# The tail of an FFT convolution kernel: reload in two portions, the last put on another queue, evictions of two banks, six outputs

## The chip, the cores and the metric

The kernel runs on one core of one Trainium2 chip. The metric is the device time of one execution in microseconds (us). Three runs of the kernel before took 263.7, 263.68 and 265.46 us, so their median is 263.7 us. The profile comes from one further execution.

## The reference

The input `x` is 1 x 224 x 224 x 96 and the filter `w` is 7 x 7 x 96 x 96, both bf16. The reference multiplies their two-dimensional spectra and transforms back, which is a circular convolution over the whole image:

```python
wp = jnp.pad(w, ((0, H - K), (0, W - K), (0, 0), (0, 0)))
Xf = rfft2(x.astype(float32), axes=(1, 2))
Wf = rfft2(wp.astype(float32), axes=(0, 1))
Yf = jnp.einsum('bhwi,hwio->bhwo', Xf, Wf)
y  = irfft2(Yf, s=(H, W), axes=(1, 2)).astype(bfloat16)
```

## The kernel before

**Tiling.** The kernel transforms along the height alone, in 8 blocks (`NJ`) of 28 output rows (`B`), to 17 frequencies (`NS`) with a real and an imaginary part each. Along the width it works directly with 7 taps, in 7 tiles (`NT`) of 32 columns, which it treats as 16 pairs (`TW`) in even and odd phase. The last tile has the index 6 (`TL`).

**Stages.** For each tile, matmuls with `Fm` take `x` to frequencies (`xf`), and VectorE makes sums and differences of them (`J`, in `jit`). `b_round(t, s, ...)` then does the products of one frequency `s`: some 33 matmuls of 96 columns into two PSUM banks, a ScalarE evacuation of the first bank (`tt__`), two VectorE operations (`u`, `v`), and a sum `yf` on GpSimd or, in some rounds, on VectorE. One round takes some 1.4 us. Every three frequencies (two at the end), the `yf` tile is written to DRAM scratch (a "put"), since the transform back needs the frequencies on the partitions. Scratch is then read back in that order in pieces of 384 bytes, multiplied by `G` (`tt` and `Gm` in the profile), evacuated by ScalarE and VectorE into `yo` or `J`, and sent to the output (`c_jobs`). For all tiles but the last, this happens in the shade of the products of later tiles.

**The last tile.** Its transform back can't lie behind another tile. Its scratch is cut at the frequencies of `SLAST` = (0, 9, 12, 15, 17). The part 0 to 9 (`scra`) is reloaded by two transfers of 480 KB when round 11 is reached (`s == SA + 2`); the parts 9 to 12, 12 to 15 and 15 to 17 (`scrb`) are reloaded by `load_b` after the last round. The puts of the last tile are collected in `puts` and issued from ScalarE's queue in a later round, except the last one, which SyncE issues. After the rounds, 12 more matmuls with `Gm` of the tile before are evacuated (the loop over `cj`). Then come

- 8 matmuls with `GA` on the first part (`first`), each 384 columns into a bank of its own;
- 26 matmuls on zeros (`WARM`) that add nothing;
- 16 matmuls with `GB` on the second part (`second`), which complete the sums, with the remaining 8 of `first` between them. Each is evacuated by `tail_evac` on one of the two engines, and each pair of 384 columns leaves as an output of 168 KB, eight outputs in all.

**Order.** The class `_Ordered` (line 89) makes each engine run its instructions in the order in which the program makes them. All compute instructions are recorded by the helper at line 99, and so all carry that line in the profile. Transfers carry one of eight completion semaphores in turn; an engine that issues a transfer first waits until the transfer that had the same semaphore before it has landed.

Of the kernel before, what the change touches and what calls it, by code (L numbers as in the profile page):

```python
# [8 lines left out]
BF16 = mybir.dt.bfloat16  # L9
F32 = mybir.dt.float32  # L10
# [4 lines left out]
B = 28  # L15
L = B + KT - 1
LC = L - 2
NS = L // 2
REAL = (0, NS - 1)
JG = 4  # L20
NJ = 8
# [12 lines left out]
PGRP = ((0, 5), (5, 8), (8, 11), (11, 14), (14, 17))  # L34
YGRP = ((0, 3), (3, 6), (6, 9), (9, 12), (12, 15), (15, 17))
YGRPL = ((0, 3), (3, 6), (6, 9), (9, 12), (12, 15), (15, 17))
SLAST = (0, 9, 12, 15, 17)
SA = SLAST[1]
YMAX = 3
YBUF = 4  # L40
JGB = ((0, 3), (3, 6), (6, 9), (9, 12), (12, 15), (15, 17))
# [23 lines left out]
def kernel(  # L65
# [50 lines left out]
    def bank():  # L116
        return pools["psb"].tile([128, 512], F32, name="pb")
# [27 lines left out]
        load["a"] += ca  # L145
        return SE.copy(out=out_ap, in_=in_ap)

    def dma(out_ap, in_ap):
        return DE.dma_start(out=out_ap, in_=in_ap)

    WF = cpool.tile([128, NSLOT, NTAP, C], BF16, name="WF")
    PP = POS * NJ
# [2 lines left out]
    xf_bufs = [cpool.tile([128, 2, 2, NS, POS, NJ], BF16, name=f"xf{i}") for i in range(2)]  # L155
    Fm = cpool.tile([R, 2, NS, JG], BF16, name="Fm")
    G = cpool.tile([3 * FR, 3 * B], BF16, name="Gm")
    KA = 4 * 2 * SA
    NL = len(SLAST) - 1
    KB = [NJ * 2 * (SLAST[i + 1] - SLAST[i]) for i in range(1, NL)]  # L160
    RB = [sum(KB[:i]) for i in range(NL - 1)]
    assert sum(KB) == 128
    XW = 2 * TW * C
    xn_bufs = [cpool.tile([R, XW + 32], BF16, name=f"xn{i}") for i in range(2)]
# [430 lines left out]
    def b_round(t, s, mid, end, ydve=False, planes=()):  # L595
# [90 lines left out]
        if s == y1 - 1:  # L686
            dst, yo0 = scr_tiles[t], 0
            if t == TL:
                i = sum(s >= v for v in SLAST[1:])
                dst, yo0 = scr_tiles[(t, i)], SLAST[i]  # L690

            def put(eng=DE):
                eng.dma_start(out=dst.rearrange("w j s e -> (w j) s e")[:, y0 - yo0:y1 - yo0],
                              in_=yf[:, 0:y1 - y0].rearrange("p s r m o -> p s (r m o)"))
            if t == TL and s < NS - 1:
                puts.append(lambda: put(SE))
            else:
                put()
# [17 lines left out]

    TW2 = 2 * TW * C
    tl_all = xf_bufs[(TL + 1) % 2].rearrange("c p r s w j -> c (p r s w j)")
    KAP = -(-KA // 16) * 16
    tl_a = [tl_all[0:KAP, g * TW2:(g + 1) * TW2].rearrange("p (w e) -> p w e", e=2 * C) for g in range(2)]  # L720
    tl_b = tl_all[:, 2 * TW2:3 * TW2].rearrange("p (w e) -> p w e", e=2 * C)

    def load_b(i):
        dma(tl_b[RB[i]:RB[i] + KB[i]], scr_tiles[(TL, 1 + i)].rearrange("w j s (r e) -> (j s r) w e", r=2))

    def g_parts():
        for g in range(2):
            for j in range(4):
                p = g * (KAP - KA) + j * 2 * SA
                dma(GA[p:p + 2 * SA, g, j * B:(j + 1) * B], G[0:2 * SA, 0:B])  # L730
                yield
        for j in range(NJ):
            for i in range(NL - 1):
                s, s1 = SLAST[i + 1:i + 3]
                n = 2 * (s1 - s)
                dma(GB[RB[i] + j * n:RB[i] + (j + 1) * n, j // 4, j % 4 * B:(j % 4 + 1) * B], G[2 * s:2 * s1, 0:B])
                yield
# [10 lines left out]
    def c_jobs(t):  # L748
        jobs = []
        w0 = t * 2 * TW  # L750
        for gi, h in LT if t < TL - 1 else LTL:
            hold = {}
            nq = 2 if gi < 2 else 3

            def mk_(q, gi=gi, h=h, nq=nq, hold=hold):
                def put(j0, nj, px, npx, row, col):
                    yo = hold["yo"]

                    def go():
                        dma(out[0, j0 * B:(j0 + nj) * B, w0 + px:w0 + px + npx, :].rearrange("h w c -> h (w c)"),  # L760
                            yo[row:row + nj * B, col:col + npx * C])
                    if tail[0] or t == TL - 1 and gi != 2:
                        outs.append(go)
                    else:
                        go()

                def f():
                    if q % 2 == 0:
                        hold["yo"] = new_yo()
                    tt = tt_tiles[(t, gi, h)]  # L770
                    yo = hold["yo"]
                    nj = 2 if q == 2 else 3
                    for b in range(2):
                        pb = bank()[0:nj * B, 0:4 * C]
                        TE.matmul(pb, lhsT=G[0:nj * FR, 0:nj * B],
                                  rhs=tt[0:nj * FR, 4 * q + 2 * b:4 * q + 2 * b + 2, :].rearrange("p w e -> p (w e)"), start=True, stop=True)
                        k = 2 * (q % 2) + b
                        evac(yo[0:nj * B, k * 4 * C:(k + 1) * 4 * C], pb, 4 * C)
                    if q == 1 and gi < 2:
                        put(gi * 3, 3, h * PXC, PXC, 0, 0)  # L780
                    elif q == 1:
                        put(6, 2, 0, 16, 0, 0)
                        for j in range(2):
                            put(6 + j, 1, 24, 8, 2 * B, j * 8 * C)
                    elif q == 2:
                        put(6, 2, 16, 8, 0, 0)
                    if q == nq - 1:
                        held[gi == 2] -= 1
                        pump()
                return f  # L790
            for q in range(nq):
                jobs.append(mk_(q))
        return jobs
# [73 lines left out]
    for r in range(NS + LAG):  # L867
# [28 lines left out]
        if r == PGRP[-2][1] + 1:  # L896
# [3 lines left out]
            t2_pool = ctx.enter_context(tc.tile_pool(name="tt2", bufs=1, side="right"))  # L900
            yo_pool = ctx.enter_context(tc.tile_pool(name="yo", bufs=2, side="right"))
            g_pool = ctx.enter_context(tc.tile_pool(name="gp", bufs=1, side="right"))
            GA = g_pool.tile([KAP, 2, 4 * B], BF16, name="GA")
            GB = g_pool.tile([128, 2, 4 * B], BF16, name="GB")
            GE.memset(GA[:], 0.0)
            GE.memset(GB[:], 0.0)
# [23 lines left out]
    gp = g_parts()  # L930
    for t in range(2, NT):
        if t == TL:
            scr_tiles[t] = None
            scr_tiles[(t, 0)] = dr_pool.tile([TW, NJ, SA, 4 * C], BF16, name="scra")
            for i in range(1, NL):
                scr_tiles[(t, i)] = dr_pool.tile([TW, NJ, SLAST[i + 1] - SLAST[i], 4 * C], BF16, name=f"scrb{i}")
        else:
            scr_tiles[t] = dr_pool.tile([TW, NJ, NS, 4 * C], BF16, name="scr")
        qs = []
# [14 lines left out]
        for s in range(NS):  # L954
            now = ()
            if s in plan:
                g = plan[s]
                now = jit(t, g + 1) if g + 1 < len(JGB) else jit(t + 1, 0)
            if s == (3 if t in (2, TL) else 2):
                queue_c(t - 1)  # L960
            if t in (3, 4):
                next(gp, None)
            if t == TL and s == SA + 2:
                sv = scr_tiles[(TL, 0)].rearrange("w j s (r e) -> (j s r) w e", r=2)
                for g in range(2):
                    dma(tl_a[g], sv[g * (2 * KA - KAP):g * (2 * KA - KAP) + KAP])
            b_round(t, s, fills(qs, 2 * s), fills(qs, 2 * s + 1), bool(now) or (t == TL and s >= NS - 3), now)
    tail[0] = 1
    load["v"], load["a"] = 1000.0, 0.0
    while cj:  # L970
        cj.pop(0)()
    assert not pend
    for i in range(NL - 1):
        load_b(i)
    for f in outs:
        f()
    if NP2:
        for c in reversed(ps_cms):
            c.__exit__(None, None, None)
        pools["psb"] = ctx.enter_context(tc.tile_pool(name="pst", bufs=8, space=bass.MemoryType.PSUM))  # L980
    M4 = 4 * B

    def first(g, q):
        pc = bank()[0:M4, 0:4 * C]
        TE.matmul(pc, lhsT=GA[:, g], rhs=tl_a[g][:, 2 * q:2 * q + 2, :].rearrange("p w e -> p (w e)"), start=True, stop=False)
        return pc

    def second(g, q, pc, yo):
        TE.matmul(pc, lhsT=GB[:, g], rhs=tl_b[:, 2 * q:2 * q + 2, :].rearrange("p w e -> p (w e)"), start=False, stop=True)
        tail_evac(yo[0:M4, q % 4 * 4 * C:(q % 4 + 1) * 4 * C], pc, 4 * C)  # L990
    order = [(g, q) for h in range(2) for g in range(2) for q in range(4 * h, 4 * h + 4)]
    live = {k: first(*k) for k in order[:8]}
    for _ in range(WARM):
        TE.matmul(live[order[7]].rearrange("p (a b) -> p a b", a=3), lhsT=wu[:, 0:M4], rhs=wu[:].unsqueeze(1).to_broadcast([128, 3, 128]),
                  start=False, stop=False)
    LF = 4
    load["v"], load["a"] = 0.0, 160.0
    for i, (g, q) in enumerate(order):
        if q % 4 == 0:
            yo = t_pool.tile([128, TW // 2, 2 * C], BF16, name="tt").rearrange("p w e -> p (w e)")  # L1000
        second(g, q, live[(g, q)], yo)
        k = i + 8 - LF
        if 8 <= k < len(order):
            live[order[k]] = first(*order[k])
        if q % 2 == 1:
            w0, c0 = TL * 2 * TW + (q - 1) * 4, (q % 4 - 1) * 4 * C
            dma(out[0, g * M4:(g + 1) * M4, w0:w0 + 8, :].rearrange("h w c -> h (w c)"), yo[0:M4, c0:c0 + 8 * C])
    if not NP2:
        ps0_cm.__exit__(None, None, None)


# [28 lines left out]
```

## Time and profile before

| quantity | value |
|---|---|
| time of the profiled execution | 263.39 us |
| its span, from the first to the last instruction | 261.7 us |
| median of three runs | 263.7 us |
| granted TensorE clock over the span | 1.000 |
| TensorE matmuls (PE), busy | 250.2 us (96%) |
| VectorE (DVE), busy | 217.7 us (83%) |
| ScalarE (ACT), busy | 196.8 us (75%) |
| GpSimd (POOL), busy | 97.9 us (37%) |
| DMA, mean rate | 179 GB/s |

PE is TensorE's matmuls, PEld its weight loads; SPq and ACTq are the transfers that SyncE and ScalarE issue. Times are in us from the start of the span; in a line of the timeline the first number is the start, the second the time until the end of the group, and `[1.80 <-...]` is the idle time ahead of it with what ended it. Groups of the timeline can overlap, since an engine starts an instruction before the one ahead has quite ended. The time lies 1.69 us above the span in this execution.

### The profile page before, as it was taken

Reading aid. Unit: us, or ns where it says so; the run is one execution under the profiler, and the core shown is the slowest. Engines: PE = TensorE matmul, PEld = TensorE weight load, DVE = VectorE, ACT = ScalarE, POOL = GpSimd, SP = SyncE. Lnnn points to the kernel's source line nnn. Section 1 sums busy time; section 2 is a strip of 40 time slices with the busy share of each in tenths; the row PEclk is TensorE's granted clock in tenths of the full one; section 3 lists DMA queues with packets and bytes.
Section 4 is the critical chain, followed back from the end, with each engine's and each line's share of the span. In section 5 each row is a group of like instructions: output and inputs, shape, how many; then the busy total and the mean of one; then the engine's idle time right before and its main releaser. Section 6 shows DMA issues by size and latency. Waiting matters only on the chain.

```text
span 261.7 us, 11972 instructions
## 1 busy us (share of the span) xinstructions
PE 250.2 (96%) x5047; PEld 232.7 (89%) x5047; DVE 217.7 (83%) x462; ACT 196.8 (75%) x470; POOL 97.9 (37%) x152
## 2 busy tenths in 40 slices
PE   8979999999998999999999999999999999989983
PEld 3979999999998999999999998999999989979662
DVE  6889999899999778778887788878989799889724
ACT  8979987787744968988988789897988853555523
POOL 7782234554655532323233322334123422423100
PEclk9999999999999999999999999999999999999999
DMA  7994105511112498998968496969859842887996
GB/s 184 275 190 121 48 6 158 158 49 48 48 49 94 146 229 147 281 278 229 281 183 244 121 260 211 237 157 288 277 168 191 279 144 79 207 215 196 243 251 202
DMA packets 47278, 46.88 MB, mean 179 GB/s; under 512 B 35696, under 2 KB 38452, under 8 KB 47224
## 3 DMA queue, kind: packets, MB, share of 16 engines
q1 hardware_dynamic: 46504, 44.64, 62.6%
q10 hardware_dynamic: 720, 1.47, 1.7%
q8 instruction: 39, 0.64, 1.0%
q14 instruction: 15, 0.12, 0.1%
HBM read 24.76 MB, written 21.33 MB: 176 GB/s over the span
## 4 chain that ended last, share of the span: by engine, by line
PE 72%; DMA 10%; DVE 8%; issue 3%; ACT 3%; SPq 1%; POOL 1%; DVEq 0%; ACTq 0%
PE pb L99 71%; DVE J L99 3%; DMA WF<-in_x_dram 3%; DVE v L99 2%; DMA tt<-scr 2%; DVE WF L99 2%; DMA xf<-scrb 2%; DMA wq<-in_w_dram 1%; SPq L99 1%; DMA scrb<-yf 1%; ACT xf L99 1%; POOL yf L99 1%; DMA scr<-yf 1%; ACT WF L99 1%; DVE u L99 1%
## 5 line engine op out<-in xcount | busy, mean ns | idle before, releaser
L99 PE MATMUL pb<-WF,J 96*128 96x96 bf16 x2821 | 162.5, 206 | 2.5 <-DVE J L99 1.6
L99 PEld LDWEIGHTS <-J 96*128 96x128 bf16 x2821 | 137.8, 98 | 11.4 <-issue 2.7
L99 POOL TENSOR_TENSOR yf<-v,u 128x384 bf16<-128x384 f32 x79 | 81.6, 1046 | 139.5 <-issue 79.4
L99 ACT CAST xf<-pb 96x408 bf16<-96x408 f32 (+6 forms) x140 | 65.2, 493 | 3.2 <-PE pb L99 1.3
L99 PE MATMUL pb<-WF,xf 96*128 96x96 bf16 x952 | 60.1, 206 | 0.9 <-DVE J L99 0.9
L99 DVE TENSOR_TENSOR J<-xf 96x456 bf16<-96x456 bf16 (+3 forms) x85 | 56.5, 704 | 0.0
L99 PEld LDWEIGHTS <-xf 96*128 96x128 bf16 x952 | 47.3, 98 | 1.4 <-ACT xf L99 0.8
L99 PE MATMUL pb<-Fm,xn 118*128 118x136 bf16 (+4 forms) x576 | 43.7, 203 | 0.2 <-ACT xf L99 0.2
L99 PE MATMUL pb<-tt,Gm 102*84 102x384 bf16 (+1 forms) x132 | 32.0, 326 | 0.5 <-DVE yf L99 0.4
L99 ACT CAST yo<-pb 84x384 bf16<-84x384 f32 (+1 forms) x61 | 26.1, 481 | 6.3 <-PE pb L99 4.5
L99 PEld LDWEIGHTS <-xn 118*128 118x128 bf16 x576 | 28.7, 98 | 0.3 <-issue 0.3
L99 ACT CAST J<-pb 84x384 bf16<-84x384 f32 (+1 forms) x64 | 27.6, 494 | 0.6 <-PE pb L99 0.6
L99 DVE TENSOR_TENSOR J<-J 96x912 bf16<-96x912 bf16 (+2 forms) x42 | 24.3, 579 | 0.0
L99 ACT CAST WF<-pb 96x480 bf16<-96x480 f32 x42 | 21.3, 566 | 0.1
L99 PEld LDWEIGHTS <-wq 128*128 128x128 bf16 (+1 forms) x288 | 19.6, 149 | 0.4 <-issue 0.4
L99 DVE TENSOR_TENSOR yf<-v,u 128x384 bf16<-128x384 f32 x26 | 15.1, 582 | 0.9
L99 PE MATMUL pb<-wq 128*128 128x120 bf16 x192 | 15.2, 224 | 0.0
L99 DVE TENSOR_TENSOR WF<-WF 96x960 bf16<-96x960 bf16 x15 | 13.7, 914 | 1.4 <-ACT WF L99 1.3
L99 PEld LDWEIGHTS <-Gm 102*84 102x84 bf16 (+1 forms) x132 | 11.4, 117 | 1.6 <-issue 0.6
L99 ACT COPY xf<-xf 96x816 bf16<-96x816 bf16 (+4 forms) x18 | 10.8, 659 | 0.0
L99 PEld LDWEIGHTS <-wu 128*112 128x112 bf16 (+1 forms) x42 | 5.5, 132 | 5.7 <-issue 3.6
L99 DVE CAST tt<-pb 112x384 bf16<-112x384 f32 x8 | 4.2, 555 | 6.5 <-PE pb L99 6.1
(397 smaller groups left out, 254.8 us busy)
## 6 DMA issues: line engine op xcount, KB each, us to landing
scr<-yf SPq DMA_DIRECT2D x30, 288.0 KB
xn<-in_x_dram SPq DMA_DIRECT2D x12, 672.0 KB
tt<-scr SPq DMA_DIRECT2D x24, 336.0 KB
out_dram<-yo SPq DMA_DIRECT2D x12, 252.0 KB
out_dram<-J SPq DMA_DIRECT2D x12, 252.0 KB
tt<-scr SPq DMA_DIRECT2D x6, 288.0 KB
wq<-in_w_dram SPq DMA_DIRECT2D x5, 288.0 KB
WF<-in_x_dram SPq DMA_DIRECT2D x2, 672.0 KB
```

Of the source, the lines that this page charges most:

```text
L99: r = fn(*a, **k)
```

## The change

1. `SLAST` becomes (0, 6, 9, 12, 15, 17), and the first `NA` = 2 parts form the operand of `first`. Part 0 to 6 is reloaded when round 8 is reached, part 6 to 9 in round 11 (`load_a`), each by two transfers; part 9 to 12 (`load_b(0)`) is reloaded in round 14. The constant matrix `GA` is filled by 16 small transfers instead of 8.
2. The last put goes into `puts` too and is issued from ScalarE (`puts.pop(0)()`) ahead of the remaining 12 evacuations; the reloads of 12 to 15 and 15 to 17 follow from SyncE. `chain` fixes the order of the last tile's transfers in the program.
3. The outputs of the tile before are issued when they are due instead of after the reloads, and two of them are merged into one (`28x2x768`).
4. The PSUM pool of eight single banks is closed and one of four two-bank tiles is opened. `first` and `second` do two matmuls of 512 columns each into such a tile, six tiles in all instead of 16 banks. `part` says where an eviction is cut between ScalarE and VectorE: both take 512 columns of the first and last tile, and one of them takes all 1024 of each tile between. Four tiles are started ahead of the 26 matmuls on zeros, the other two behind the second and third pair.
5. The results go into `J_bufs` and leave by six outputs of 224 KB each.

```diff
-SLAST = (0, 9, 12, 15, 17)
-SA = SLAST[1]
+SLAST = (0, 6, 9, 12, 15, 17)
+NA = 2
+SA = SLAST[NA]
...
-            if t == TL and s < NS - 1:
+            if t == TL:
                 puts.append(lambda: put(SE))
...
+    def load_a(i):
+        sv = scr_tiles[(TL, i)].rearrange("w j s (r e) -> (j s r) w e", r=2)
+        for g in range(2):
+            r0 = g * (2 * KG[i] - KP[i])
+            dma(tl_a[g][RA[i]:RA[i + 1]], sv[r0:r0 + KP[i]])
...
-                    if tail[0] or t == TL - 1 and gi != 2:
+                    if tail[0]:
                         outs.append(go)
...
-            if t in (3, 4):
+            if t in (3, 4, 5):
                 next(gp, None)
-            if t == TL and s == SA + 2:
-                sv = scr_tiles[(TL, 0)].rearrange("w j s (r e) -> (j s r) w e", r=2)
-                for g in range(2):
-                    dma(tl_a[g], sv[g * (2 * KA - KAP):g * (2 * KA - KAP) + KAP])
+            if t == TL:
+                for i in range(NA):
+                    if s == SLAST[i + 1] + 2:
+                        load_a(i)
+                if s == SLAST[NA + 1] + 2:
+                    load_b(0)
...
     tail[0] = 1
+    puts.pop(0)()
+    assert not puts
     load["v"], load["a"] = 1000.0, 0.0
     while cj:
         cj.pop(0)()
-    for i in range(NL - 1):
+    for i in range(1, NL - NA):
         load_b(i)
     for f in outs:
         f()
+    for c in reversed(ps_cms) if NP2 else [ps0_cm]:
+        c.__exit__(None, None, None)
+    pools["psb"] = ctx.enter_context(tc.tile_pool(name="pst", bufs=4, space=bass.MemoryType.PSUM))
...
+    HC = 512
     def first(g, q):
-        pc = bank()[0:M4, 0:4 * C]
-        TE.matmul(pc, lhsT=GA[:, g], rhs=tl_a[g][:, 2 * q:2 * q + 2, :].rearrange("p w e -> p (w e)"), start=True, stop=False)
+        pc = pools["psb"].tile([128, 2, HC], F32, name="pc")
+        for b in range(2):
+            TE.matmul(pc[0:M4, b], lhsT=GA[:, g], rhs=fl[g][:, (2 * q + b) * HC:(2 * q + b + 1) * HC], start=True, stop=False)
         return pc
+    def second(g, q, pc, part):
+        for b in range(2):
+            TE.matmul(pc[0:M4, b], lhsT=GB[:, g], rhs=fl[2][:, (2 * q + b) * HC:(2 * q + b + 1) * HC], start=False, stop=True)
+        a = pc[0:M4].rearrange("p b n -> p (b n)")
+        o = yl[g][:, 2 * q * HC:2 * (q + 1) * HC]
+        if part:
+            apart(("T", g, q), 0, SE.copy(out=o[:, 0:part], in_=a[:, 0:part]))
+        if part < 2 * HC:
+            apart(("T", g, q), 1, VE.tensor_copy(out=o[:, part:], in_=a[:, part:]))
-    live = {k: first(*k) for k in order[:8]}
+    live = {k: first(*k) for k in order[:4]}
     for _ in range(WARM):
...
     for i, (g, q) in enumerate(order):
-        second(g, q, live[(g, q)], yo)
-        k = i + 8 - LF
-        if 8 <= k < len(order):
-            live[order[k]] = first(*order[k])
+        second(g, q, live[(g, q)], (HC, 2 * HC, 0, 2 * HC, 0, HC)[i])
+        if 0 < i < 3:
+            live[order[i + 3]] = first(*order[i + 3])
```

More of the change, by code (lines that the diff above doesn't have):

```diff
@@ L146, in tail_evac, with dma @@
         return SE.copy(out=out_ap, in_=in_ap)
-    def dma(out_ap, in_ap):
-        return DE.dma_start(out=out_ap, in_=in_ap)
+    chain = []
+    def dma(out_ap, in_ap, eng=DE):
+        r = eng.dma_start(out=out_ap, in_=in_ap)
+        if chain:
+            if chain[-1]:
+                tc.add_manual_dep(r.ins, chain[-1].ins.name, NOSYNC, reason="transfers in program order")
+            chain.append(r)
+        return r
     WF = cpool.tile([128, NSLOT, NTAP, C], BF16, name="WF")
@@ L157 @@
     G = cpool.tile([3 * FR, 3 * B], BF16, name="Gm")
-    KA = 4 * 2 * SA
     NL = len(SLAST) - 1
-    KB = [NJ * 2 * (SLAST[i + 1] - SLAST[i]) for i in range(1, NL)]
-    RB = [sum(KB[:i]) for i in range(NL - 1)]
+    KG = [4 * 2 * (SLAST[i + 1] - SLAST[i]) for i in range(NA)]
+    KP = [-(-k // 16) * 16 for k in KG]
+    RA = [sum(KP[:i]) for i in range(NA + 1)]
+    KB = [NJ * 2 * (SLAST[i + 1] - SLAST[i]) for i in range(NA, NL)]
+    RB = [sum(KB[:i]) for i in range(NL - NA)]
     assert sum(KB) == 128
@@ L692, in put @@
             def put(eng=DE):
-                eng.dma_start(out=dst.rearrange("w j s e -> (w j) s e")[:, y0 - yo0:y1 - yo0],
-                              in_=yf[:, 0:y1 - y0].rearrange("p s r m o -> p s (r m o)"))
-            if t == TL and s < NS - 1:
+                dma(dst.rearrange("w j s e -> (w j) s e")[:, y0 - yo0:y1 - yo0],
+                    yf[:, 0:y1 - y0].rearrange("p s r m o -> p s (r m o)"), eng)
+            if t == TL:
                 puts.append(lambda: put(SE))
@@ L718 @@
     tl_all = xf_bufs[(TL + 1) % 2].rearrange("c p r s w j -> c (p r s w j)")
-    KAP = -(-KA // 16) * 16
-    tl_a = [tl_all[0:KAP, g * TW2:(g + 1) * TW2].rearrange("p (w e) -> p w e", e=2 * C) for g in range(2)]
+    tl_a = [tl_all[0:RA[NA], g * TW2:(g + 1) * TW2].rearrange("p (w e) -> p w e", e=2 * C) for g in range(2)]
     tl_b = tl_all[:, 2 * TW2:3 * TW2].rearrange("p (w e) -> p w e", e=2 * C)
+    def load_a(i):
[3 more added lines that the diff above has]
+            dma(tl_a[g][RA[i]:RA[i + 1]], sv[r0:r0 + KP[i]])
     def load_b(i):
-        dma(tl_b[RB[i]:RB[i] + KB[i]], scr_tiles[(TL, 1 + i)].rearrange("w j s (r e) -> (j s r) w e", r=2))
+        dma(tl_b[RB[i]:RB[i] + KB[i]], scr_tiles[(TL, NA + i)].rearrange("w j s (r e) -> (j s r) w e", r=2))
     def g_parts():
-        for g in range(2):
[L728 to L731, printed above, removed]
+        for i in range(NA):
+            s, s1 = SLAST[i:i + 2]
+            n = 2 * (s1 - s)
+            for g in range(2):
+                for j in range(4):
+                    p = RA[i] + g * (KP[i] - KG[i]) + j * n
+                    dma(GA[p:p + n, g, j * B:(j + 1) * B], G[2 * s:2 * s1, 0:B])
+                    yield
         for j in range(NJ):
-            for i in range(NL - 1):
-                s, s1 = SLAST[i + 1:i + 3]
+            for i in range(NL - NA):
+                s, s1 = SLAST[NA + i:NA + i + 2]
                 n = 2 * (s1 - s)
@@ L782, in f @@
                         put(6, 2, 0, 16, 0, 0)
-                        for j in range(2):
-                            put(6 + j, 1, 24, 8, 2 * B, j * 8 * C)
+                        if t == TL - 1:
+                            dma(out[0, 6 * B:8 * B, w0 + 24:w0 + 32, :].rearrange("(j h) w c -> h j (w c)", j=2),
+                                hold["yo"][2 * B:3 * B].rearrange("p (j q) -> p j q", j=2))
+                        else:
+                            for j in range(2):
+                                put(6 + j, 1, 24, 8, 2 * B, j * 8 * C)
                     elif q == 2:
@@ L902 @@
             g_pool = ctx.enter_context(tc.tile_pool(name="gp", bufs=1, side="right"))
-            GA = g_pool.tile([KAP, 2, 4 * B], BF16, name="GA")
+            GA = g_pool.tile([RA[NA], 2, 4 * B], BF16, name="GA")
             GB = g_pool.tile([128, 2, 4 * B], BF16, name="GB")
@@ L932 @@
         if t == TL:
+            chain.append(None)
             scr_tiles[t] = None
-            scr_tiles[(t, 0)] = dr_pool.tile([TW, NJ, SA, 4 * C], BF16, name="scra")
-            for i in range(1, NL):
-                scr_tiles[(t, i)] = dr_pool.tile([TW, NJ, SLAST[i + 1] - SLAST[i], 4 * C], BF16, name=f"scrb{i}")
+            for i in range(NL):
+                scr_tiles[(t, i)] = dr_pool.tile([TW, NJ, SLAST[i + 1] - SLAST[i], 4 * C], BF16, name=f"scrl{i}")
         else:
@@ L960 @@
                 queue_c(t - 1)
-            if t in (3, 4):
+            if t in (3, 4, 5):
                 next(gp, None)
-            if t == TL and s == SA + 2:
-                sv = scr_tiles[(TL, 0)].rearrange("w j s (r e) -> (j s r) w e", r=2)
-                for g in range(2):
-                    dma(tl_a[g], sv[g * (2 * KA - KAP):g * (2 * KA - KAP) + KAP])
+            if t == TL:
+                for i in range(NA):
+                    if s == SLAST[i + 1] + 2:
+                        load_a(i)
+                if s == SLAST[NA + 1] + 2:
+                    load_b(0)
             b_round(t, s, fills(qs, 2 * s), fills(qs, 2 * s + 1), bool(now) or (t == TL and s >= NS - 3), now)
     tail[0] = 1
+    puts.pop(0)()
+    assert not puts
     load["v"], load["a"] = 1000.0, 0.0
@@ L972 @@
     assert not pend
-    for i in range(NL - 1):
+    for i in range(1, NL - NA):
         load_b(i)
@@ L976 @@
         f()
[L977 to L980, printed above, removed]
+    for c in reversed(ps_cms) if NP2 else [ps0_cm]:
+        c.__exit__(None, None, None)
+    pools["psb"] = ctx.enter_context(tc.tile_pool(name="pst", bufs=4, space=bass.MemoryType.PSUM))
     M4 = 4 * B
+    HC = 512
+    yl = [J_bufs[g][0:M4, 0:TW2] for g in range(2)]
+    fl = [v.rearrange("p w e -> p (w e)") for v in tl_a + [tl_b]]
@@ L983, in first @@
     def first(g, q):
-        pc = bank()[0:M4, 0:4 * C]
-        TE.matmul(pc, lhsT=GA[:, g], rhs=tl_a[g][:, 2 * q:2 * q + 2, :].rearrange("p w e -> p (w e)"), start=True, stop=False)
-        return pc
[L988 to L991, printed above, removed]
@@ L993 @@
+    order = [(g, q) for q in range(TW2 // (2 * HC)) for g in range(2)]
+    live = {k: first(*k) for k in order[:4]}
     for _ in range(WARM):
[L994 to L997, printed above, removed]
+        TE.matmul(live[order[3]][0:M4, 1, 0:384].rearrange("p (a b) -> p a b", a=3), lhsT=wu[:, 0:M4],
+                  rhs=wu[:].unsqueeze(1).to_broadcast([128, 3, 128]), start=False, stop=False)
@@ L998 @@
     for i, (g, q) in enumerate(order):
-        if q % 4 == 0:
-            yo = t_pool.tile([128, TW // 2, 2 * C], BF16, name="tt").rearrange("p w e -> p (w e)")
-        second(g, q, live[(g, q)], yo)
-        k = i + 8 - LF
-        if 8 <= k < len(order):
-            live[order[k]] = first(*order[k])
-        if q % 2 == 1:
-            w0, c0 = TL * 2 * TW + (q - 1) * 4, (q % 4 - 1) * 4 * C
-            dma(out[0, g * M4:(g + 1) * M4, w0:w0 + 8, :].rearrange("h w c -> h (w c)"), yo[0:M4, c0:c0 + 8 * C])
@@ L1008 @@
-    if not NP2:
-        ps0_cm.__exit__(None, None, None)
+        second(g, q, live[(g, q)], (HC, 2 * HC, 0, 2 * HC, 0, HC)[i])
+        if 0 < i < 3:
+            live[order[i + 3]] = first(*order[i + 3])
+        c0 = 2 * q * HC
+        dma(out[0, g * M4:(g + 1) * M4, TL * 2 * TW:(TL + 1) * 2 * TW, :].rearrange("h w c -> h (w c)")[:, c0:c0 + 2 * HC], yl[g][:, c0:c0 + 2 * HC])
 _INS = ['x', 'w']
```

## The prediction

> **What bounds the kernel now.** I read the totals and the clock first, then the chain of work that ended last, then the timeline of its last 28 us.
>
> ```profile
> span 261.7 us, 11972 instructions
> PE 250.2 (96%) x5047; PEld 232.7 (89%) x5047; DVE 217.7 (83%) x462; ACT 196.8 (75%) x470; POOL 97.9 (37%) x152
> PEclk9999999999999999999999999999999999999999
> ```
>
> TensorE is busy nearly throughout at full clock, and the change leaves its products alone. What can move is the tail, which the chain shows:
>
> ```profile
> 237.98 6.47 PE pb L99 x135
> 244.45 0.55 DVE yf L99
> ...
> 245.01 3.39 DMA scrb<-yf
> ...
> 248.42 4.44 DMA xf<-scrb
> ...
> 253.00 3.96 PE pb L99 x22
> ...
> 256.98 0.56 DVE tt L99
> ```
>
> After the last sum `yf` (ends 244.99) the path is a put of 3.39 us, a reload of 4.44, and the matmuls with `GB`, which start at 253.00. So the change seems to aim well. But TensorE has other work between 245 and 253, and the timeline shows how little room that leaves:
>
> ```profile
> 234.17 0.34 ACTq L99 DMA_DIRECT2D scra<-yf  x1
> 234.60 0.85 ACT L99 CAST yo<-pb 56x384 bf16<-56x384 f32 x2 [1.80 <-DMA out_dram<-J]
> ...
> 239.40 0.33 ACTq L99 DMA_DIRECT2D scrb<-yf  x1
> 239.85 0.41 ACT L99 ACTIVATE tt__7221<-pb 128x288 f32<-128x288 f32 x1 [1.63 <-PE pb L99]
> ...
> 243.28 0.33 ACTq L99 DMA_DIRECT2D scrb<-yf  x1
> ...
> 243.91 2.00 ACT L99 CAST J<-pb 84x384 bf16<-84x384 f32 x5
> 245.76 0.91 ACT L99 CAST yo<-pb 84x384 bf16<-84x384 f32 x2
> ```
> ```profile
> 240.85 0.34 DVE L99 SCALAR_TENSOR_TENSOR u<-pb,tt__7221 128x192 f32<-128x192 f32 x1
> ...
> 246.30 1.00 DVE L99 CAST yo<-pb 84x384 bf16<-84x384 f32 x2
> 247.52 4.39 PE L99 MATMUL pb<-wu 128*112 128x384 bf16 x26
> ...
> 253.37 4.63 DVE L99 CAST tt<-pb 112x384 bf16<-112x384 f32 x8 [6.07 <-PE pb L99]
> 254.04 4.68 SPq L99 DMA_DIRECT2D out_dram<-tt  x8
> ```
>
> The 26 matmuls on zeros end at 247.52 + 4.39 = 251.91, only 1.09 us before 253.00. They stand in the program ahead of the matmuls with `GB`, and the change keeps all 26. Whatever starts them more than 1.09 us later takes over the path from the reload.
>
> **Step 1: the reload.** The put and the last reload lose company: the parts up to 12 are read earlier, so only 12 to 15 is under way with them. The put has 3.39 us as a ceiling; as a floor I take 2.3, the time from the last output's issue (258.40) to its landing as the completion events show it (260.70). The reload has 4.44 as a ceiling, and as a floor 2.3 and half of 512 pieces at 2.2 ns (the DMA view counts 2,058 such packets from 247 to 251.5; half, since landing and moving overlap): 2.9. So the data are there at 244.99 + 5.2 to 7.8 = 250.2 to 252.8, at best 2.7 us earlier than now. This counts only if TensorE is ready by then.
>
> **Step 2: the last put in ScalarE's queue.** In the built program it stands ahead of ScalarE's seven evacuations for the tile before, and it waits for the last `yf`. Now these evacuations start at 243.91, while SyncE does the waiting. Then they queue behind the put: 244.99 + 0.02 for the issue, 0.33 for its length, and some 0.11 to the next instruction (243.28 + 0.33 to the copy at 243.70 is 0.09): 245.46, that is 1.55 later. They run one per 0.37 us already ((245.76 - 243.91)/5), so nothing is made up, and the last ends at 246.67 + 1.55 = 248.22 instead of 246.67. VectorE's last one ends at 247.30 (246.30 + 1.00) and hardly moves.
>
> The row for such holding is the cast at 234.60, which sat idle 1.80 us and started 0.43 behind the start of the put at 234.17. [...]
>
> **Step 3: the new PSUM pool.** The single banks are closed and two-bank tiles opened. In the built program the first matmul with `GA` waits for the last evacuation of ScalarE and its weight load for the last one of VectorE, and no later one of these eight waits for either. Before, each waited for its own bank, so they started at 245.85 among the evacuations. Now: 248.22 + 0.05 = 248.27.
>
> **Step 4: to the matmuls with `GB`.** Matmuls of 384 columns follow each other every (4.39 - 0.33)/25 = 0.162 us, so one of 512 costs 0.217. Eight of them and 26 on zeros: 8 x 0.217 + 26 x 0.162 = 1.73 + 4.22. Start: 248.27 + 5.95 = 254.22 against 253.00, **+1.2 us**. The reload (by 252.8) is then hidden. Bounds: +0.3, if only VectorE's last evacuation counted (247.35 + 5.95 = 253.30), to +1.6, if ScalarE's queue lost another 0.4.
>
> **Step 5: from there to the end.** Before, 16 evictions end 5.0 us after the start (253.37 + 4.63), the last output is issued at 258.40 (+5.4), and the span ends at +8.7. After: an eviction from a two-bank tile shows early in this kernel as 96x800, 985 ns on VectorE and 822 on ScalarE; with 555 and 481 ns for 384 columns the slopes are 1.03 and 0.82 ns per column, so 1024 columns cost 1.22 and 1.01 us, 512 some 0.69 and 0.59. The first pair of matmuls ends at 0.43, its evictions start at 0.64 (0.2 behind, as 253.37 against 253.00 + 0.16) and end at 1.32. The built program then makes the fifth `first` wait for these evictions (it gets their banks), and the third pair stands behind it: 1.37 + 4 x 0.217 = 2.24. So VectorE's 1024 run from 2.44 to 3.66. The sixth `first` waits for ScalarE's 1024 (to 2.2); pairs four to six end at 3.1, 3.5 and 4.0; VectorE's second 1024 run from 3.7 to 4.95 and its last 512 to 5.55, half a microsecond later than before, though there are 9 eviction parts instead of 16. The last output is 224 KB instead of 168, some 0.1 us more. **+0.65 us.** Bounds: without the two stalls VectorE needs 0.64 + 3.55 = 4.2, so -0.8; if the two-bank evictions overlap less, +0.9.
>
> **Step 6: the earlier reload of 0 to 6.** It now enters the queue behind the reload of 233.11 at some 233.5. The put of part 9 to 12 (239.40 now) waits in ScalarE's queue for the completion semaphore that the second of these transfers holds. Ahead of its landing lie some 1.4 MB (that reload, 0.59 MB of the new one, a put, outputs); the two stages like it moved at 208 GB/s (222.5 to 229) and 233 GB/s (239.5 to 246). [...] VectorE wants `tt__7221` at 240.85 and ScalarE has it at 240.26, so 0.55 us are free; beyond that each late microsecond passes on, since VectorE is busy almost without a gap from 240.85 to 244.99. Cost 0 to 1.3 us; I take **+0.5**, the case of the middle.
>
> **Step 7: the rest.** Eight more tiny fills of `GA` and `GB` cost SyncE some 0.33 us each, spread over tile 5, whose rounds TensorE fills; one output less saves one such issue. Outputs issued early lie under the rounds. Nothing, at most +0.3 if a reload for a `Gm` matmul slipped behind them.
>
> **Sum.** 1.2 + 0.65 + 0.5 = +2.35 us on 263.39, that is 265.7 for an execution like the profiled one. That one lies 0.3 below the median of 263.7, so I forecast **266.0 us**: slower, by some 0.9%.
>
> **The rivals.**
> - *The semaphore holds ScalarE longer* (slower still). If step 6's second transfer takes the 7.3 us that the second `scra` reload took (issued 239.10, landed 246.39), it lands at 241.2 and costs 1.3: with steps 4 and 5 this is 263.7 + 3.15 = 266.9. For it: both stages of such reloads ran that slowly. Against: 590 KB here, 960 KB there.
> - *The casts are not held* and only the pool counts: 253.30, +0.3, with steps 5 and 6 some 265.1. For it: nothing in ScalarE's rows.
> - *The reload decides* (not slower). If TensorE had its 5.95 us of fillers behind it when the data land at, say, 250.7, the tail would begin 2.3 us earlier: 263.7 - 2.3 + 0.65 = 262.1; with step 5 at its lower bound 260.6. The point from which it decides: the first `GA` matmul must start by 250.7 - 5.95 = 244.75. Against: the last cast of VectorE alone ends at 247.30.
> - *The stalls of step 5 don't occur* (the change works there as its eviction count promises): -0.8 in place of +0.65, so 264.6.
>
> **Chances.** My forecast 0.50, the longer hold 0.22, no held casts 0.08, the reload 0.06, no stalls 0.14. The forecast's own range, 265.0 to 266.7, and the neighbours make the range 264.2 to 267.6, which leaves out the reload case and the extremes. Some 1% (2.6 us) is what a measurement of this kernel tells from no change: three runs lay 1.8 apart. Above 266.3 lie three tenths of my own case and most of the longer hold, 0.36 with a little of the rest; below 261.1 only the best of the reload case, 0.03; within 0.61.
>
> **What would show it.** Right: no idle time of PE ahead of the first `GB` matmul with a DMA as releaser; the matmuls on zeros run up to it, and the ScalarE casts start some 0.45 us behind an ACTq put at 245 or later. Idle PE ahead of the fifth and sixth `GA` pair, released by evictions, shows step 5. An ACTq put of 9 to 12 later than 239.9 shows step 6. Wrong: `GB` matmuls that start before 253, or wait for a reload.

## The result, and the profile after

The change makes the kernel slower. The changed kernel took 273.43 us, the median of six runs (270.65 to 275.29), against 264.42 us for the kernel before. Runs that lie more than 1.5% above the fastest of the same kernel are left out of the ratio, which is 1.0258 (95% interval 1.0219 to 1.0298). The profiled execution took 270.65 us, with a span of 268.9 us: 7.2 more than before. The forecast was 266.0, and 267.6 the end of its range.

The page of the changed kernel, its totals and the clock:

```profile
span 268.9 us, 11955 instructions
...
PE 253.3 (94%) x5039; PEld 232.6 (87%) x5039; DVE 217.7 (81%) x458; ACT 196.3 (73%) x466; POOL 98.6 (37%) x152
...
PEclk9999999999999999999999999999999999999598
```

TensorE runs eight matmuls fewer and is yet busy 3.1 us longer. The digit 5 near the end of the clock's row says why: for a stretch there the granted clock was half. The chain that ended last:

```profile
250.38 9.54 PE pc L100 x36
...
260.00 0.70 DVE J L100
...
260.74 2.38 PE pc L100 x10
...
263.15 1.23 DVE J L100
```

Before, put and reload stood here; now TensorE's matmuls with `GA`, on zeros and with `GB` form one block of 9.54 us. The timeline shows what started it so late:

```profile
234.70 0.88 SPq L100 DMA_DIRECT2D xf<-scrl  x2
...
241.10 0.85 SPq L100 DMA_DIRECT2D xf<-scrl  x2
...
241.98 0.34 ACTq L100 DMA_DIRECT2D scrl<-yf  x1
...
242.44 0.41 ACT L100 ACTIVATE tt__7232<-pb 128x288 f32<-128x288 f32 x1 [3.70 <-PE pb L100]
...
242.96 0.36 DVE L100 SCALAR_TENSOR_TENSOR u<-pb,tt__7232 128x192 f32<-128x192 f32 x1 [1.63 <-ACT tt__7232 L100]
...
246.56 0.55 DVE L100 TENSOR_TENSOR yf<-tt__7361,pb 128x384 bf16<-128x384 f32 x1
...
247.07 3.52 SPq L100 DMA_DIRECT2D xf<-scrl  x3
...
247.13 0.34 ACTq L100 DMA_DIRECT2D scrl<-yf  x1
...
247.57 1.99 ACT L100 CAST J<-pb 84x384 bf16<-84x384 f32 x5 [1.44 <-DVE J L100]
248.44 1.02 DVE L100 CAST yo<-pb 84x384 bf16<-84x384 f32 x2
249.43 0.89 ACT L100 CAST yo<-pb 84x384 bf16<-84x384 f32 x2
250.38 3.57 PE L100 MATMUL pc<-xf,GA 80*112 80x512 bf16 x8 [1.58 <-ACT yo L100]
...
253.74 5.73 PE L100 MATMUL pc<-wu 128*112 128x384 bf16 x26
...
259.31 1.03 PE L100 MATMUL pc<-xf,GB 128*112 128x512 bf16 x4
```

Three things can be read here. The put of part 9 to 12 starts at 241.98 instead of 239.40, and VectorE idles 1.63 us for the copy behind it. The casts start 0.44 us behind the last put, and the first `GA` matmul waits for the last cast. The eight `GA` matmuls then take 3.36 us (250.38 to 253.74) and the zeros 5.57 (to 259.31), against 1.73 and 4.22 as priced for full clock (a3, below, measures 1.74 and 4.23). Busy times by windows of 3.41 us show the clock itself (columns: stretch, its length, busy PE, PEld, DVE, ACT, POOL, granted clock, DMA share, GB/s):

```profile
246.23:249.64 3.41, 1.71 (x7) 0.68 (x6) 3.23 (x7) 2.07 (x6) 0.00 (x0) 1.00 0.61 200
249.64:253.05 3.41, 2.67 (x7) 1.42 (x8) 0.00 (x0) 0.68 (x2) 0.00 (x0) 0.50 1.17 220
253.05:256.46 3.41, 3.41 (x12) 2.13 (x11) 0.00 (x0) 0.00 (x0) 0.00 (x0) 0.50 0.47 183
256.46:259.87 3.41, 3.41 (x22) 2.65 (x21) 0.00 (x0) 0.00 (x0) 0.00 (x0) 1.00 0.00 0
```

TensorE was busy 1.71 of 3.41 us, then the clock halved at 249.64 and came back at 256.46. Of these 6.82 us, 6.08 lie behind the start at 250.38; half of them, 3.0 us, is lost.

### The profile page after: what moved, and what is told of

It is laid out like the page before. It is cut to its first block, busy times and chain, and to the rows that moved or that the text cites. A ratio compares the mean times of both kernels' runs of the same rounds, so it can differ in the third digit from the quotient of the medians.

```text
span 268.9 us, 11955 instructions
## 1 busy us (share of the span) xinstructions
PE 253.3 (94%) x5039; PEld 232.6 (87%) x5039; DVE 217.7 (81%) x458; ACT 196.3 (73%) x466; POOL 98.6 (37%) x152
## 5 line engine op out<-in xcount | busy, mean ns | idle before, releaser
L100 PEld LDWEIGHTS <-J 96*128 96x128 bf16 x2821 | 137.7, 98 | 11.6 <-issue 2.9
L100 PE MATMUL pb<-tt,Gm 102*84 102x384 bf16 (+1 forms) x132 | 33.2, 326 | 1.9 <-DVE u L100 0.8
L100 DVE CAST J<-pc 112x512 bf16<-112x512 f32 (+1 forms) x4 | 3.7, 956 | 11.8 <-PE pc L100 11.7
L100 ACT CAST J<-pc 112x512 bf16<-112x512 f32 (+1 forms) x4 | 3.0, 802 | 10.9 <-issue 9.7
```

What stands on the lines that cost most here:

```text
L100: r = fn(*a, **k)
```

## The experiments

Twelve kernels were run. All are read by four distances in the profiled execution, which add up to the span's difference: how late VectorE was already at 239.8 of the kernel before (a lag that arises ahead of the tail: by 106 us in all kernels but c1; it is no effect of an edit alone, since before, b1, b2 and c3 run the same program up to there and show 0, 0.8, 0.3 and 0), what is added to that by 240.8 (the hold), the time from the end of the last `yf` to the first `GB` matmul, and the time from there to the end.

| kernel | lag | hold | `yf` to `GB` | `GB` to end | ratio of runs (95%) |
|---|---|---|---|---|---|
| before | 0 | 0 | 8.0 | 8.7 | 1 |
| after | 0.4 | 1.7 | 12.2 | 9.6 | 1.0258 (1.0219 to 1.0298) |
| a1 last put on SyncE | 1.1 | 1.3 | 11.2 | 9.5 | 1.0238 (1.0139 to 1.0338) |
| a2 first part in one portion | 2.6 | 0 | 12.0 | 10.0 | 1.0266 (1.0174 to 1.0359) |
| a3 zeros as fillers | 1.7 | 1.6 | 9.3 | 9.6 | 1.0158 (1.0053 to 1.0263) |
| a4 no zeros | -0.2 | 1.9 | 7.0 | 11.6 | 1.0118 (1.0030 to 1.0206) |
| b1 before, last put on ScalarE | 0.8 | 0 | 7.7 | 8.7 | 1.0004 (0.9974 to 1.0035) |
| b2 before, new tail | 0.3 | 0 | 8.4 | 9.7 | 1.0089 (1.0047 to 1.0131) |
| b3 before, early reload | 3.3 | 0 | 7.6 | 9.0 | 0.9984 (0.9950 to 1.0018) |
| b4 b3 with 18 zeros | 0.1 | 0 | 8.2 | 9.0 | 1.0022 (0.9992 to 1.0052) |
| c1 after, reload one round later | 7.6 | 0 | 12.4 | 9.5 | 1.0187 (1.0136 to 1.0238) |
| c2 c1 in single banks, 18 zeros | 0.1 | 0 | 7.5 | 8.8 | 0.9923 (0.9886 to 0.9960) |
| c3 b2 with fillers | 0 | 0 | 11.0 | 9.7 | 1.0130 (1.0085 to 1.0176) |
| c4 after, old tail | 2.1 | 1.6 | 8.9 | 8.7 | 1.0119 (1.0079 to 1.0160) |

**The clock: a3, a4 and c3.** a3 puts matmuls on zeros where TensorE idles, behind each of the twelve closing matmuls with `Gm`; a4 takes the 26 away; c3 does in b2 what a3 does in the changed kernel.

```diff
+for i in range(FILL if tail[0] else 0):   # FILL = 2
+    TE.matmul(pb..., lhsT=wu[:, 0:nj * B], rhs=wu..., start=False, stop=i == FILL - 1)
```

> The kernel after, with 24 more matmuls on zeros: two behind each of the 12 matmuls whose evacuations close the tile before, so that TensorE is not idle between 243.6 and 250.4; they add zeros to the same sums. Theory (the half clock comes from this idle stretch): the granted clock stays at 1.00, the 8 GA matmuls take 1.7 us instead of 3.4 and the 26 on zeros 4.2 instead of 5.4, so 3 us less: 267.7 us, or 268.2 if the fillers delay the casts by half a microsecond. Rival (the clock falls for another reason): no change or slower, 270.7 to 272.

> The kernel after without the 26 matmuls on zeros. Theory (they, and not the reload, stand in the path): the GB matmuls start when the GA matmuls are done, near 254, where the reload lands too (253.7 in the profile after), 5.4 us earlier; the tail behind then runs at half clock and loses 1 to 2 us: 266.3 to 267.3 us. Rival (the reload is the path and the matmuls on zeros fill time that is waited anyway): 270.7 or more, since the tail at half clock comes on top.

The timeline of a3:

```profile
251.61 1.91 PE L101 MATMUL pc<-xf,GA 80*112 80x512 bf16 x8 [0.69 <-ACT yo L101]
...
253.35 4.39 PE L101 MATMUL pc<-wu 128*112 128x384 bf16 x26
...
257.58 1.03 PE L101 MATMUL pc<-xf,GB 128*112 128x512 bf16 x4
```

The first `GA` matmul starts 3.37 us behind the last `yf`, as in the changed kernel (3.27), but the granted clock is 1.00 in every window, and `GB` comes 9.3 instead of 12.2 us behind it. Only TensorE's own work was added, so in this execution the idle TensorE cost those 2.9 us. The fillers don't show as clearly in the runs: the three others had mean clocks of 0.973, 0.983 and 0.995, without a trace that says where they lost it, and the intervals of the two ratios overlap. a4 had half clock from 246.04 to 259.69, nearly the end of its matmuls: `GB` waits for the reload then, 7.0 us behind the `yf`, and the end takes 11.6 instead of 9.6. It still beats the changed kernel: the zeros had been put in the path.

> The kernel before with the new tail alone, and two matmuls on zeros added behind each of the twelve closing matmuls, so that TensorE is not idle there. Theory (the new tail costs 1.4 us at full clock, and what it costs beyond that is a clock that falls in most of the executions): executions near 265 as the fastest ones of the new tail alone, granted clock near that of the kernel before, and the slower cluster 2 to 4 us above thins out; median some 2 us below that of the new tail alone. Rival (the spread has another cause, such as the transfers): same spread and same median as the new tail alone.

This one missed its forecast of the time: a median of 268.0 us against 268.3 for b2, where some 2 less was expected. Its six executions had a clock of 0.994 to 0.999, b2's twelve 0.971 to 0.994, as the theory says. The spread shows nothing: c3's six lie within 3.0 us and b2's twelve 9.2 apart, but without the five of b2 above 269 us its spread is 3.4. And the fillers made the closing casts slower, a pair each 0.98 us, so `GA` started 5.05 us behind the `yf` instead of 2.42, which ate the gain.

**The hold: a2 and c1.** a2 sets `SLAST = (0, 9, 12, 15, 17)`, `NA = 1`. c1 issues the reload of 0 to 6 one round later, so that the put of 9 to 12 takes another of the eight semaphores:

```diff
-if s == SLAST[i + 1] + 2:
+if s == SLAST[i + 1] + (3 if i == 0 else 2):
     load_a(i)
```

> The kernel after, with one part undone: the first scratch part is 0 to 9 again, reloaded by one pair of transfers in round 11; the early reload of 9 to 12 and all else stay. In the built program the put of 9 to 12 then gets the semaphore of a much older transfer. Theory: ScalarE issues that put at 239.4 to 239.8 instead of 241.98 and the last sum ends 1.7 to 2.1 us earlier; the half clock stays if TensorE's idle stretch does: 268.7 us; if the clock stays up too, some 265.7. Rival (the two-portion reload is harmless): 270.7, no change against the kernel after.

> The changed kernel with one edit: the reload of part 0 to 6 is issued one round later, behind the two J outputs of the tile before, so that the put of part 9 to 12 takes a completion semaphore whose transfer has long landed. Theory (this semaphore held ScalarE by 1.7 us): the put of 9 to 12 starts at some 239.5 and the last yf ends at 245.0 to 245.4, -1.7 us on the changed kernel; whether TensorE then keeps its clock is open (-3 more if it does). Rival (the hold is load on the transfers, not a semaphore): the put stays at 241 or later and the time unchanged.

The timeline of c1, whose profiled execution fell 7.6 us behind between 181 and 210 us of the kernel before (in its own time its clock was half from 204.26 to 211.09):

```profile
247.02 0.33 ACTq L100 DMA_DIRECT2D scrl<-yf  x1
247.47 0.41 ACT L100 ACTIVATE tt__7232<-pb 128x288 f32<-128x288 f32 x1 [1.95 <-POOL yf L100]
```

The put is 247.02 - 239.40 = 7.62 behind that of before, exactly the lag: no hold is left, in c1 as in a2. In all five kernels with the reload of 0 to 6 in round 8 it is 1.3 to 1.9 us, in none of the other nine does it exist. Since c1 moves the same bytes, it was the semaphore, whose transfer landed at 241.91 in the changed kernel, 0.07 ahead of the put. In c1 the reload of 0 to 6 was still under way when the put started, and landed 3.15 us later, at 250.17, so a reload under way does not by itself hold the put. The clock still halved in both. By the ratios c1 is 0.7% below the changed kernel, 1.9 us where 1.7 was expected, though the intervals overlap. In a2 nothing shows in the ratio; its profiled execution had a larger early lag.

**The last put: a1 and b1.** a1 takes it off ScalarE in the changed kernel (`if t == TL and s < NS - 1:`, and no `puts.pop(0)()` after the rounds); b1 puts it there in the kernel before.

> The kernel after, with one part undone: SyncE issues the last put again, so ScalarE's seven evacuations don't queue behind it. Theory (three separate holds, and a half clock that follows from the idle TensorE): the ScalarE casts end some 1.4 us earlier, but VectorE's last cast (249.46 in the profile after) then releases the GA matmuls, so they start 0.9 us earlier, at about 249.5; the half clock stays, since TensorE is as idle ahead of them: 269.8 us. If the shorter gap is enough to keep the clock, 266.8. Rival (the put in ScalarE's queue is the whole cause): back to the time before, some 264.

> The kernel before with the last put moved to ScalarE's queue and nothing else. Theory (the put holds ScalarE's seven casts by 1.5 us, and this counts only together with the two-bank pool, which waits for all of them): the last cast ends at some 248.2 instead of 246.7, the matmuls on zeros end at some 252.9, still about when the reload lands, so GB starts at 253.0 to 253.4 and the time is +0.0 to +0.5 us. Rival A (the thinner stretch of TensorE ahead of the casts alone is enough to halve the clock): the zeros run at half clock, +2.5 to +3.5 us. Rival B (the casts are held without harm and the put starts earlier from its own queue): -0.3.

In a1 the first `GA` matmul starts 2.43 us behind the `yf` instead of 3.27, 0.8 earlier, but the clock halves all the same. In b1 the casts are held too (they start at 246.18, 0.36 behind the put), and it costs nothing: in single banks the `GA` matmuls start at 247.25 between the casts, and the clock stays.

**The tail: b2 and c4.** b2 is the kernel before with the new code from the PSUM pool on; c4 is the changed kernel with the old code there.

> The kernel before with the new tail alone (two-bank pool, 512 columns a matmul, cut evictions, six outputs); puts and reloads as before. Theory (the new pool makes the GA matmuls wait for the last evacuation, and the idle TensorE ahead of them halves the clock): GA starts 2.4 us after the last sum, PEclk falls to half behind it, GA and zeros take 9 us instead of 6, and the time is +0.3 for the wait, +3 for the clock and +0.9 for the evictions, some +4.2 us (268). Rival (the clock falls only because the earlier reload has thinned the rounds as well): full clock, +0.3 and +0.9, so +1.2 us (265.5).

> The changed kernel with the tail alone undone (single banks, 384 columns, eight outputs, 26 matmuls on zeros); reloads, puts and their queues stay as changed. Theory: the hold of 1.7 us stays, the casts are held by the last put, but the GA matmuls run among them and TensorE is not left idle; GB starts 7.8 us behind the last yf as with the put alone on ScalarE, +1.5 us against the kernel before and 5 us less than the changed kernel. Rival (the hold of the rounds alone empties TensorE enough): half clock here too, +4 to +5.

b2's profiled execution kept its clock and was the fastest of twelve: 0.4 us for the later `GA` and 1.0 at the end, where the prediction has 0.65. One other lay 0.2 us above it; ten were 1.8 to 9.2 us slower, nine of them with less granted clock. But for seven of these nine that was 0.989 or 0.990 instead of 0.994, by the clock alone (its shortfall times the span) some 1.0 to 1.4 us, where they were 1.8 to 7.1 us slower. So the expectation at full clock describes the profiled execution; that a half clock in the tail made the others slower isn't shown, since only one was traced. c4 fell between its two: hold 1.6, and half clock for one window instead of two:

```profile
247.49:250.90 3.41, 2.42 (x12) 1.21 (x11) 3.38 (x8) 1.99 (x6) 0.00 (x0) 1.00 0.57 153
250.90:254.31 3.41, 3.41 (x12) 2.25 (x11) 0.14 (x1) 0.98 (x3) 0.00 (x0) 0.50 0.75 177
```

So the hold, which thins out the last rounds, can drain TensorE without the new tail, and the new tail without the hold.

**The earlier reload: b3, b4 and c2.** b3 is the changed kernel in one portion, with the last put on SyncE and the old tail; b4 has 18 zeros in it. c2 is c1 with the old tail and `WARM = 18`.

> The kernel before with the reload of part 9 to 12 moved from behind the rounds to round 14, and the outputs of the tile before issued when due; the first part stays in one portion, the last put on SyncE, the tail in single banks. Theory (the earlier reload shortens the path from the last sum to the data from 7.9 to some 6.6 us, holds nothing as the first part is not cut, and leaves TensorE's stretch as it was): zeros end at some 251.9 at full clock, GB starts there instead of at 253.0, -1.0 us. Rival A (the zeros or the put decide anyway): 0. Rival B (the earlier reload also holds ScalarE's queue by a semaphore): +1.3 or more, with the clock lost perhaps +4.

> As the early reload alone, but with 18 instead of 26 matmuls on zeros, to let GB start as soon as the data have landed. Theory: zeros end at some 250.6, the data land at some 251.5, clock stays full, -1.4 us against the kernel before. Rival (the idle gap of about 1 us ahead of GB, or the lesser warming, costs the clock): GB and the evictions run at half clock, about +1 us on the early reload alone.

> A version that is meant to beat both: the same later reload of 0 to 6, the last put on ScalarE, but the tail in single banks as before and 18 matmuls on zeros. Theory: the last yf ends as before (245.0), the data land 6.6 us behind it as in the changed kernel (251.6), zeros end at 245.0 + 3.4 + 2.9 = 251.3, GB starts at 251.6 instead of 253.0, -1.4 us against the kernel before. Rival A (the path from the last sum to the data is set by how many bytes are still to be moved, and stays near 7.9): 0. Rival B (the clock falls): +2 or more.

b3 and b4 gained nothing. The timeline of SyncE's queue in b4, with the last `yf` ready at 245.12, shows why:

```profile
245.60 0.30 SPq L100 DMA_DIRECT2D xf<-scrl  x1
...
245.96 0.66 SPq L100 DMA_DIRECT2D scrl<-yf  x1
...
248.09 2.42 SPq L100 DMA_DIRECT2D xf<-scrl  x2
```

The "early" reload of 9 to 12 isn't early. It waits for the put of 9 to 12, which was issued at 239.52 behind the big reload and landed at 245.54, six microseconds later; and the last put stands behind it. Neither of my theories for these two had that. c2, with the put on ScalarE, is the version that beats both: by the ratio it is 0.8% ahead of the kernel before, and as medians of all runs 263.43 us against 264.68. Its timeline:

```profile
245.16 0.33 ACTq L100 DMA_DIRECT2D scrl<-yf  x1
...
246.64 2.06 PE L100 MATMUL pb<-xf,GA 80*112 80x384 bf16 x8
...
248.54 3.09 PE L100 MATMUL pb<-wu 128*112 128x384 bf16 x18
...
253.02 4.63 DVE L100 CAST tt<-pb 112x384 bf16<-112x384 f32 x8 [5.53 <-PE pb L100]
```

The zeros end at 251.63 and the data land at 252.51, 7.4 us behind the `yf`, not 6.6: rival A for the most part. This profile shows 0.5 us of gain in that distance; the ratio says 2.0 (1.1 to 3.0), the medians 1.25. Where the rest comes from stays open.

## Why the prediction was wrong

The direction was right and the size was a third of the truth: +2.35 us forecast on the profiled execution, +7.2 measured. The terms are 0.4 of early lag, 1.7 of hold, 1.2 and 3.0 up to `GB`, and 0.9 at the end.

- *Step 4 failed.* The eight matmuls and 26 on zeros were priced at full clock, 5.95 us; they took 8.93. I had forecast an idle TensorE ahead of them and never asked what clock follows. The 1.2 us from the later start are there as forecast. No rival had the clock either. TensorE's idle times around the drop at 249.64 were short: the longest was 1.58 us (until 250.38), and in c4, which dropped at 250.90, 0.76.
- *Step 6 was mis-sized.* 0.5 us, bounds 0 to 1.3; it was 1.7. The mechanism is shown by c1. The transfers entered the queue at 234.70 instead of 233.5, since they first waited for a put, and the second took some 7 us to 241.91: the rival "longer hold" had that duration, but not the later issue. The step's 0 to 1.3 counts with 0.7 us from the last packet to the landing, which no run shows; at the end of the kernel before, the last packet ends at 260.38 and its transfer lands at 260.70, 0.32 later.
- *Steps 2 and 3 held.* `GA` started 3.27 us behind the last `yf`, forecast 3.28; the casts began 0.44 behind the put, forecast 0.45. But b1 shows that the held casts cost nothing without the two-bank pool (ratio 1.0004).
- *Step 1 held by its number, not by its reason.* The data were there 6.6 us behind the `yf` (5.2 to 7.8 forecast), at 253.68, long before `GB`. But the part 9 to 12 was reloaded at 247.07, together with the rest, as in b4, so the put kept its company (3.14 us, before 3.39); the last reload took 3.39 instead of 4.44.
- *Step 5 held roughly.* 0.94 instead of 0.65, above its upper bound of 0.9 by a little, with the forecast stall of the fifth pair visible. The step's lower bound was added up wrongly: VectorE's four parts at its own prices are 2 x 1.22 + 2 x 0.69 = 3.82 us, not 3.55, so the bound is -0.5 and the rival without stalls 264.9.
- *Step 7 held.* The lag stays at 0.37 to 0.52 from 222 to 239.8.

## What to carry to other kernels

Before you price the matmuls behind a wait, add up how busy TensorE is in the microseconds before them; here, with 1.71 of 3.41 us busy, the eight `GA` matmuls took 3.36 us, and in a3, with the idle times filled, 1.74. The pool that is closed and opened anew turned many small waits into one for the last release (the first `GA` matmul started 3.27 us behind the last `yf`, before 0.86): keep single banks where other engines still drain them. And for a transfer that is issued on an engine with other work, look up which transfer held its completion semaphore last (here for 1.7 us), and when the data of an "earlier" reload are really written (in b4 the put landed six microseconds after its issue).

## What was not expected of the hardware

The half clock around the last matmuls lasted 6.83 us in the changed kernel, a1, a2 and c1, 3.41 in c4 and 13.65 in a4: two, one and four times 3.41. In the changed kernel the granted clock changed at 249.64, 256.46 and 266.70 us, 6.83 and 10.24 apart (2 and 3 times 3.413), and in c1 at 204.26, 211.09, 255.46 and 262.29, 6.83, 44.37 and 6.83 apart (2, 13 and 2 times). The drop falls elsewhere in each trace: at 248.56 in a1, 249.73 in a2, 246.04 in a4 and 250.90 in c4.

In the 3.41 us ahead of the drop TensorE was busy 1.38 us (c1), 1.71 (after), 1.92 (a1), 2.13 (a2), 2.23 (a4) and 2.42 (c4). Busy time alone doesn't decide it: 3.41 us with 2.09 in b2 (246.35 to 249.76) and 1.49 in b4 (249.24 to 252.65) had full clock, and full clock behind them. Nor does the longest idle time: it was 0.76 us in c4, and in b4 TensorE idled 2.61 us up to 253.34 at a granted clock of 1.00. What sets off the half clock, and why b2's profiled execution escaped it, is not shown by these runs.
